# Chunk 0's loop in a hand-written engine order, paired weight conversions and a later output-weight conversion

## The chip, the cores and the metric

The program runs on one core of one Trainium2 chip. The metric is the device time of one execution in microseconds (us). The engines are TensorE (PE in the profile), VectorE (DVE), ScalarE (ACT), GpSimd (POOL) and SyncE (SP), whose queue issues nearly all DMAs.

## The reference, cut to what matters

```python
# 4 x 8 heads, 576 positions, head dim 64; window of 128 keys, linear position bias
scores = where(mask, q @ k.T / 8 + bias, -1e9)
x = softmax(scores) @ v                      # -> 2304 tokens x 512
x = ((x @ w_a) * (x @ w_b)) @ w_out          # float64 weights, 512 x 1536, 512 x 1536, 1536 x 512
logits = x @ w_gate + modality_bias[modality_id]
e = argmax(logits); gate = max softmax prob
out[token] = gate * (relu(x @ w1[e]) @ w2[e])   # 8 experts, 512 x 1024 x 512
```

Products in float32 quality are made of three reduced-precision products (high x high, high x low, low x high), so most operands exist as a high and a low half.

## The kernel before, in words

The 2304 tokens are 18 blocks of 128, grouped into seven **chunks** of 3, 2, 2, 3, 3, 3 and 2 blocks (`CH`, line 43). Attention runs ahead of the product with the gated weights: an **item** is one block of one pair of heads, four pairs to a chunk, so chunk 0 has items 0 to 11 (`n0` is 12), chunk 1 items 12 to 19, and chunk 2 starts with item 20. An item is a score product (`score_mm`), a masked maximum on VectorE (`score_sel`, `score_max`), two exponentials on ScalarE (`score_exp`), the inverse sums on VectorE (`score_inv`), two transposes (`pt_tr`), a copy on ScalarE and two triangular selects on GpSimd (`pt_cp`), the product with the values (`pv_mm`), its scaling out of PSUM (`pv_ev`, tile `u`), and a transpose and copy into the x of the next stage (`pv_tr`, `pv_x`).

The **prologue** (lines 826 to 920) does chunk 0's items in a hand-written order, three items in flight, with the loads and the first weight conversions woven in (`conv_step`).

After it, each chunk runs 12 **steps** j (`NJ`): `mm_ab(c, j, 0)` and `mm_ab(c, j, 1)` are the products with pair j of the weights a and b (12 matmuls each), the result of the first is copied by ScalarE (`asb`), VectorE multiplies it with the second (`gf`), and `mm_out` adds its product with row block j of the output weights to accumulators, one step later. While chunk 0 runs, the weights are made as well. They arrive as float64: per weight, three VectorE operations build the float32 bits (`f64_ops`, lines 452 to 470), ScalarE rounds the high half and VectorE subtracts it for the low half (`f64_split`, line 472). For pair j that is six operations, two casts and two subtractions over 128x512; the output weights need the three operations only, and are written to DRAM for the later chunks (`WoOps`).

What sets the order: chunks 1 to 5 are inside a block in which TensorE, ScalarE and VectorE take the order of the code (`step`, line 1107). Chunk 0's loop (`slot0`, line 1045) is not: there a scheduler with a timeline of its own places instructions, led by priorities (`HP0`, `HPO`) and by `issue_after`. GpSimd and SyncE are always placed by the scheduler, outside the prologue. In `slot0(j)` the output weights of step j + 1 and the pair j + 2 are converted; items go on at eight in twelve steps, and so do the preparations of keys, queries and values of the items ahead (`a_preps`).

## Time and profile before

| | |
|---|---|
| median of 3 runs (lowest, highest) | 841.86 us (840.77, 845.12) |
| profiled execution: its own time, its span | 843.18 us, 840.9 us |
| busy share of the span: PE, DVE, ACT, POOL | 97%, 65%, 55%, 28% |
[...]

The span runs from the first to the last instruction; the rest of the profiled execution's own time lies around it. A busy share is an average over stages with different limits, so the sections below read stretches of the span. A duration in a row includes some 0.1 us in which the next instruction of that engine already runs, so the step from start to start is shorter than the mean of one.

### The profile page before, as it was taken

Reading aid. Unit: us, or ns where it says so; the run is one execution under the profiler, and the core shown is the slowest. Engines: PE = TensorE matmul, PEld = TensorE weight load, DVE = VectorE, ACT = ScalarE, POOL = GpSimd, SP = SyncE. Lnnn points to the kernel's source line nnn. Section 1 sums busy time; section 2 is a strip of 40 time slices with the busy share of each in tenths; the row PEclk is TensorE's granted clock in tenths of the full one; section 3 lists DMA queues with packets and bytes.
Section 4 is the critical chain, followed back from the end, with each engine's and each line's share of the span. In section 5 each row is a group of like instructions: output and inputs, shape, how many; then the busy total and the mean of one; then the engine's idle time right before and its main releaser. Section 6 shows DMA issues by size and latency. Waiting matters only on the chain.

```text
span 840.9 us, 14490 instructions
## 1 busy us (share of the span) xinstructions
PE 813.1 (97%) x4726; PEld 728.0 (87%) x4726; DVE 546.7 (65%) x1619; ACT 461.2 (55%) x1149; POOL 236.1 (28%) x349
## 2 busy tenths in 40 slices
PE   8899999999999999999999999999999999999994
PEld 6788877898898899999999899988988998989893
DVE  7799993677766676767777776468476544447320
ACT  6744453777677766667667643232345443547420
POOL 5422010533344333243333421210133130115001
PEclk9999999999999999999999999999999999999998
DMA  9995443567655675564455544458428564549301
GB/s 252 336 399 193 141 141 113 170 197 230 173 164 152 207 179 154 157 167 136 135 157 152 134 131 119 117 160 272 153 66 305 203 195 136 164 137 295 119 27 40
DMA packets 77348, 144.61 MB, mean 172 GB/s; under 512 B 13839, under 2 KB 40623, under 8 KB 77264
## 3 DMA queue, kind: packets, MB, share of 16 engines
q1 hardware_dynamic: 73712, 133.86, 52.6%
q0 software_dynamic: 3552, 9.73, 3.2%
q8 instruction: 40, 0.66, 0.3%
q14 instruction: 44, 0.36, 0.1%
HBM read 118.16 MB, written 22.12 MB: 167 GB/s over the span
## 4 chain that ended last, share of the span: by engine, by line
PE 65%; DMA 9%; ACT 8%; issue 8%; DVE 5%; POOL 2%; SPq 1%; POOLq 0%; ACTq 0%; DVEq 0%
PE ps_ab L539 26%; PE acc L556 10%; PE ps_h L1291 9%; PE ps_y L1274 8%; PE acc L552 4%; PE ps_o L412 2%; PE ps_s L268 2%; DMA wraw<-in_moe_w_b 2%; ACT u L419 2%; DMA kk<-in_k 1%; ACT p L292 1%; DMA x2d<-x 1%; ACT qq L200 1%; PE ps_p L327 1%; DMA qr<-in_q 1%
## 5 line engine op out<-in xcount | busy, mean ns | idle before, releaser
L539 PE MATMUL ps_ab<-xr,wab 128*128 128x384 f32 (+1 forms) x2016 | 339.2, 318 | 3.3 <-DVE gf L1243 1.6
L539 PEld LDWEIGHTS ps_ab<-xr,wab 128*128 128x128 f32 x2016 | 309.1, 189 | 12.1 <-issue 2.2
L556 PE MATMUL acc<-wo,g 128*128 128x512 f32 x540 | 138.7, 398 | 1.5 <-ACT g L1156 1.5
L556 PEld LDWEIGHTS acc<-wo,g 128*128 128x128 f32 x540 | 96.6, 188 | 20.6 <-ACT g L1156 2.3
L1291 PE MATMUL ps_h<-xT,w1s 128*128 128x384 f32 x576 | 105.7, 340 | 0.0
L1274 PE MATMUL ps_y<-w2s,h 128*128 128x512 f32 x432 | 104.1, 394 | 0.0
L343 POOL TENSOR_SCALAR_AFFINE_SELECT pt<-pc 128x512 fp32r<-128x512 f32 (+1 forms) x72 | 53.8, 747 | 176.0 <-DVE pc L341 109.8
L1291 PEld LDWEIGHTS ps_h<-xT,w1s 128*128 128x128 f32 x576 | 101.1, 190 | 0.9
L1274 PEld LDWEIGHTS ps_y<-w2s,h 128*128 128x128 f32 x432 | 79.7, 188 | 15.8
L292 ACT ACTIVATE p<-p,mx 128x128 f32<-128x128 f32 x144 | 57.0, 398 | 55.1 <-DVE mx L282 55.0
L1144 DVE TENSOR_TENSOR gf<-ps_ab,asb 128x384 f32<-128x384 f32 (+1 forms) x60 | 30.3, 504 | 64.4 <-PE ps_p L327 43.4
L637 DVE CUSTOM_DVE_ANT_0 junk<-x,wgt 128x512 f32<-128x512 f32 x88 | 62.6, 711 | 8.9 <-DMA wgt<-in_wgt 4.2
L423 POOL TENSOR_TENSOR xf<-u 128x128 f32<-128x128 f32 x52 | 25.6, 492 | 128.5 <-ACT u L419 128.5
L310 ACT ACTIVATE p<-p,mx 128x128 f32<-128x128 f32 x104 | 36.5, 397 | 37.2 <-DVE mx L299 37.2
L955 DVE TENSOR_TENSOR w2s<-wr,w2s 128x1024 fp32r<-128x1024 f32 x24 | 29.4, 1225 | 38.4 <-ACT w2s L954 38.1
L1281 POOL DMA_INDIRECT out<-y,idx x18 | 21.2, 1178 | 113.7 <-ACT y L1280 112.2
L419 ACT COPY u<-ps_o 64x384 f32<-64x384 f32 x104 | 49.5, 476 | 3.2 <-PE ps_o L412 2.0
L345 POOL TENSOR_SCALAR_AFFINE_SELECT pt<-pc 128x512 fp32r<-128x512 f32 (+1 forms) x72 | 49.9, 693 | 0.0
L1294 ACT ACTIVATE h<-ps_h 128x384 fp32r<-128x384 f32 x48 | 23.6, 492 | 45.4 <-PE ps_h L1291 43.0
L955 DVE TENSOR_TENSOR w1s<-wr,w1s 128x1024 fp32r<-128x1024 f32 x28 | 34.3, 1224 | 19.0 <-ACT w1s L954 16.3
L1123 ACT COPY asb<-ps_ab 128x384 f32<-128x384 f32 (+1 forms) x60 | 25.9, 431 | 33.9 <-PE ps_ab L539 33.7
L1295 DVE SCALAR_TENSOR_TENSOR h<-ps_h,h 128x384 fp32r<-128x384 f32 x48 | 26.4, 555 | 27.9 <-ACT h L1294 27.9
(224 smaller groups left out, 1231.1 us busy)
## 6 DMA issues: line engine op xcount, KB each, us to landing
wo<-wo_d SPq DMA_DIRECT2D x60, 512.0 KB
wr<-in_moe_w SPq DMA_DIRECT2D x56, 512.0 KB
wgt<-in_wgt SPq DMA_DIRECT2D x32, 256.0 KB
wraw<-in_moe_w_a SPq DMA_DIRECT2D x12, 512.0 KB
wraw<-in_moe_w_b SPq DMA_DIRECT2D x12, 512.0 KB
wor<-in_moe_w_out SPq DMA_DIRECT2D x12, 512.0 KB
wo_d<-wo SPq DMA_DIRECT2D x12, 512.0 KB
kr<-in_k SPq DMA_DIRECT2D x24, 256.0 KB
```

The costliest lines, as they stand in the source:

```text
L292: nc.scalar.activation(out=it.p[:, h, :], in_=it.p[:, h, :], func=AF.Exp, bias=it.mx[:, 2 + h:3 + h], scale=-1.0, accum_out=it.mx[:, 4 + h ...
L310: nc.scalar.activation(out=it.p[:, h, :], in_=it.p[:, h, :], func=AF.Copy, scale=it.mx[:, 6 + h:7 + h])
L343: nc.gpsimd.affine_select(out=it.pt[:, :, 0], in_=pc, pattern=pat + [[-1, P]], base=0, channel_multiplier=1, compare_op=ALU.is_gt, fill=0.0)
L345: mark["pt"] = nc.gpsimd.affine_select(out=it.pt[:, :, 1], in_=pc, pattern=pat + [[1, P]], base=0, channel_multiplier=-1, compare_op=ALU.i ...
L419: nc.scalar.copy(out=u[o:o + 64], in_=ps[o:o + 64, 1 - h:4 - h])
L539: nc.tensor.matmul(ps[:, :n], lhsT=w[:, m, r, kk * P:(kk + 1) * P], rhs=xr[:, s, kk, :n], start=(idx == 0), stop=(idx == len(terms) - 1))
L552: nc.tensor.matmul(acc[c, t], lhsT=g[:, t * P:(t + 1) * P], rhs=w, start=(j == 0), stop=(j == NJ - 1))
L556: nc.tensor.matmul(acc[c, t], lhsT=g[:, r, t * P:(t + 1) * P], rhs=w[:, s, :], start=(j == 0 and idx == 0), stop=(j == NJ - 1 and idx == 2))
L637: nc.vector.tensor_tensor_reduce(out=junk, in0=x2[:, 0:DM], in1=w, scale=1.0, scalar=0.0, op0=ALU.mult, op1=ALU.add, accum_out=lgr[:, e:e ...
L955: nc.vector.tensor_tensor(out=dst[:, 1], in0=srcw, in1=dst[:, 0], op=ALU.subtract)
L1274: nc.tensor.matmul(pss[t], lhsT=h[:, r, f, t * P:(t + 1) * P], rhs=W2[f // 2][:, s_, f % 2, :], start=(f == 0 and i == 0), stop=(f == 7 an ...
L1291: nc.tensor.matmul(ps, lhsT=W1[f // 2][:, r, kk, (f % 2) * P:(f % 2 + 1) * P], rhs=xT[:, s_, kk, :], start=(kk == 0 and i == 0), stop=(kk ...
```

## The change

Chunk 0's loop moves into the hand-ordered block of chunks 1 to 5: `slot0` goes, `step0` takes its place, and the block now opens at chunk 0 (TensorE, VectorE, ScalarE). Both weights of a pair become one tile `f64f` of 128x1024 with one buffer (it shares its place with the later gate weights `wgt`), so that a pair is three conversions, one cast and one subtraction. `step0(j)` converts the output weights of step j - 1 (before: j + 1 in slot j) and loads one step ahead less. The prologue converts pair 0 alone, from its fifth item on (`CVS` 4), and no output weights; pair 1 is converted at the head of step 0. In the prologue both halves of `u` come from ScalarE; before, VectorE made the first. Items and preparations of chunk 0's loop follow a list `goal`, as in the later chunks.

```diff
-    CVS = 1
+    CVS = 4
 def pv_ev(it):
         for h in range(2):
-            if it.a.c == 0 and h == 0:
-                nc.vector.tensor_scalar(out=it.o[:, h], in0=it.po[:, h, 0:D],
-                                        scalar1=it.mx[:, 6 + h:7 + h], scalar2=None, op0=ALU.mult)
-                continue
             nc.scalar.activation(out=it.o[:, h], in_=it.po[:, h, 0:D], func=AF.Copy,
                                  scale=it.mx[:, 6 + h:7 + h])
 def wab_jobs(j):
+        def f():
+            if not st:
+                st.append(m1.tile([P, 2 * KD * P], U32, tag="ff", bufs=1, name="f64f"))
+            return st[0]
+        def hi():
+            wab[j] = wab_p.tile([P, 2, 2, KD * P], F32R, tag=f"wab{j}", name=f"wab{j}")
+            nc.scalar.copy(out=wab[j][:, :, 0], in_=f().bitcast(F32).rearrange("p (m n) -> p m n", m=2))
+        def rest():
+            nc.vector.tensor_tensor(out=wab[j][:, :, 1], in0=f().bitcast(F32).rearrange("p (m n) -> p m n", m=2),
+                                    in1=wab[j][:, :, 0], op=ALU.subtract)
+        return f64_ops(wraw[j].rearrange("p m k f t -> p (m k f) t"), f) + [hi, rest]
...
+    def step0(j, pend, sc, tp):
+        n, last = CH[0] * P, j == NJ - 1
+        new = list(range(cur["s"], goal[j]))
+        its = [live[g] for g in tp]
+        for g in sc:
+            score_inv(live[g])
+        for i in ((1, 2) if j == 0 else (j + 2,)):
+            if i < NJ:
+                job[i] = wab_jobs(i)
+        jo = [f for i in ((j - 1, j) if last else (j - 1,)) if i >= 0 for f in wo_jobs(i)]
+        if j == 0:
+            for f in job.pop(1):
+                f()
+        elif j + 1 in job:
+            job.pop(j + 1)[4]()
+        psa = mm_ab(0, j, 0, None if j else 1)
...
+        nc.scalar.copy(out=asb[:, :n], in_=psa[:, :n])
+        for it in its:
+            xf_new(it.a)
+            pv_mm(it)
+            pv_ev(it)
+        for f in jo:
+            f()
+        js = job.get(j + 2, [])
+        for f in js[:2]:
+            f()
+        psb = mm_ab(0, j, 1)
...
+        nc.vector.tensor_tensor(out=gf[:, :n], in0=psb[:, :n], in1=asb[:, :n], op=ALU.mult)
+        for it in its:
+            pv_tr(it)
+            pv_x(it, 0)
+        for g in sc:
+            pt_tr(live[g])
+        for g in new:
+            c_, hp_, t_ = items[g]
+            live[g] = score_mm(pairs[c_, hp_], t_)
+        for f in js[2:3]:
+            f()
+        for g in sc:
+            pt_cp(live[g])
...
+        for g in new:
+            score_red(live[g])
+            score_exp(live[g])
+        for f in js[3:4]:
+            f()
+        new_preps(goal[j + 2], goal[j])
+        if pend is not None:
+            mm_out(*pend, wo_t[j - 1])
```

Three places of the order. First ScalarE in the prologue, items 3 and 4: `pc` is the transposed weights of an item copied out of PSUM, `p,mx` its exponentials, `u` its scaled product with the values, `xr` the high half of x.

```order
 L333 COPY pc<-ps_p 128x256
 L292 ACTIVATE p,mx<-p,mx 128x128 x2
-L376 ACTIVATE u<-ps_o,mx 128x64
-L392 CAST xr_131<-ps_ot 128x128
-L333 COPY pc<-ps_p 128x256
-L292 ACTIVATE p,mx<-p,mx 128x128 x2
+L372 ACTIVATE u<-ps_o,mx 128x64 x2
+L388 CAST xr_131<-ps_ot 128x128
+L333 COPY pc<-ps_p 128x256
+L292 ACTIVATE p,mx<-p,mx 128x128 x2
```

The order is the same, with two halves of `u` on this engine in the place of one.

Second, VectorE in step 2 of the loop, as it stands now (`f64f` is the pair being converted, `f64o` the output weights, `wor` their raw load, `ps_s` and `p,mx` the new item):

```order
L457 SCALAR_TENSOR_TENSOR f64f<-wraw_209,f64f 128x1024
L276 COPY_PREDICATED ps_s<-upper,ps_s 128x2x128
L282 ISA p,mx<-ps_s,m_base 128x128
L298 TENSOR_SCALAR mx<-mx 128x2
L299 RECIPROCAL mx<-mx 128x2
L483 TENSOR_TENSOR wab_838<-f64f,wab_838 128x2x512
L453 TENSOR_SCALAR f64o<-wor 128x512
L457 SCALAR_TENSOR_TENSOR f64o<-wor,f64o 128x512 x2
L453 TENSOR_SCALAR f64f<-wraw_690 128x1024
L457 SCALAR_TENSOR_TENSOR f64f<-wraw_690,f64f 128x1024
L1056 TENSOR_TENSOR gf<-ps_ab_884,asb 128x384
```

Between the new item's maximum (L282) and the subtraction of the pair (L483) the engine has only the two small operations of the inverse. Before, two pairs were in work at once, and their conversions stood between the parts of an item:

```order
L458 TENSOR_SCALAR f64f<-wraw_716 128x512
L276 COPY_PREDICATED ps_s<-upper,ps_s 128x2x128
L458 TENSOR_SCALAR f64f<-wraw_826 128x512
L462 SCALAR_TENSOR_TENSOR f64f<-wraw_716,f64f 128x512
L282 ISA p,mx<-ps_s,m_base 128x128
L462 SCALAR_TENSOR_TENSOR f64f<-wraw_826,f64f 128x512
L466 SCALAR_TENSOR_TENSOR f64f<-wraw_716,f64f 128x512
L1076 TENSOR_TENSOR gf<-ps_ab_955,asb 128x384
```

Third, ScalarE around steps 0 and 1 as it stands now; `pc` on the second row is item 12, `u` on the fifth too, `qq` the queries of the next pair of heads:

```order
L292 ACTIVATE p,mx<-p,mx 128x128 x2
L333 COPY pc<-ps_p 128x256
L480 CAST wab_720<-f64f 128x2x512
L1044 COPY asb<-ps_ab_649 128x384
L372 ACTIVATE u<-ps_o,mx 128x64 x2
L384 COPY xf_0_728<-ps_o 128x128
L333 COPY pc<-ps_p 128x256
L480 CAST wab_766<-f64f 128x2x512
L242 ACTIVATE qq<-qr_1_695,qscale 64x256 x2
L1044 COPY asb<-ps_ab_779 128x384
```

The cast of a pair (L480), which waits for VectorE's three operations, now stands ahead of `asb` and `u` of the same step.

## Rows read from the trace of the kernel before

**Rows 1.** The page: busy time and share of the span, by engine.
```profile
PE 813.1 (97%) x4726; PEld 728.0 (87%) x4726; DVE 546.7 (65%) x1619; ACT 461.2 (55%) x1149; POOL 236.1 (28%) x349
```

**Rows 2.** Busy time of each engine by stretch, clock, DMA share and GB/s.
```profile
core 0: us, PE busy (x) PEld busy (x) DVE busy (x) ACT busy (x) POOL busy (x), PEclk, DMA share, GB/s
10.00:40.00 30.00, 26.01 (x164) 20.48 (x164) 25.24 (x113) 23.21 (x89) 13.36 (x33) 1.00 1.01 319
...
59.00:142.00 83.00, 83.00 (x406) 66.35 (x405) 72.38 (x167) 37.84 (x103) 10.26 (x13) 1.00 0.49 158
142.00:212.00 70.00, 67.73 (x498) 62.68 (x498) 47.68 (x163) 52.90 (x146) 29.04 (x42) 1.00 0.63 197
```

**Rows 3.** The same view, single stretches around the loop's start.
```profile
40.00:42.00 2.00, 2.00 (x9) 2.00 (x9) 0.57 (x2) 0.47 (x2) 0.00 (x0) 0.50 0.98 384
48.00:50.00 2.00, 0.93 (x5) 0.48 (x4) 2.00 (x4) 2.00 (x8) 0.67 (x2) 1.00 1.02 410
```

**Rows 4.** Timeline of TensorE (start, us, what): chunk 0's first product.
```profile
40.22 3.15 PE L539 MATMUL ps_ab<-xr,wab 128*128 128x384 f32 x9
```

**Rows 5.** The chain that ended last, in order of time (start, us, what).
```profile
55.33 0.11 PE ps_p L327
...
68.83 0.92 PE ps_s L264 x4
...
110.63 0.47 PE ps_s L268 x4
...
118.19 0.84 PE ps_o L366 x8
...
130.10 2.58 PE acc L552 x6
132.67 4.17 PE ps_ab L539 x24
...
141.99 1.44 PE ps_ab L539 x12
```

**Rows 6.** Waits of ScalarE to 142 us: us in total, times, longest.
```profile
ACT u L376 <- DVE u L373: 6.1, 7, 1.3
```

**Rows 7.** Timeline of ScalarE, item 7 of the prologue.
```profile
26.43 0.29 ACT L376 ACTIVATE u<-ps_o,mx 128x64 f32<-128x64 f32 x1
26.62 0.25 ACT L392 CAST xr<-ps_ot 128x128 fp32r<-128x128 f32 x1
27.00 0.37 ACT L333 COPY pc<-ps_p 128x256 f32<-128x256 f32 x1
27.26 0.40 ACT L292 ACTIVATE p<-p,mx 128x128 f32<-128x128 f32 x1
...
28.05 1.13 ACT L473 CAST wab<-f64f 128x512 fp32r<-128x512 f32 x2
30.21 0.32 ACT L376 ACTIVATE u<-ps_o,mx 128x64 f32<-128x64 f32 x1 [1.03 <-DVE u L373]
```

**Rows 8.** Timeline of ScalarE: queries scaled, 64x256 and 64x384.
```profile
23.96 1.26 ACT L242 ACTIVATE kk<-raw,qscale 64x384 f32<-64x384 f32 x2
...
33.03 1.04 ACT L242 ACTIVATE qq<-qr,qscale 64x256 f32<-64x256 f32 x2
```

**Rows 9.** Timeline of GpSimd around the modality constants; then one DMA stretch.
```profile
18.97 0.21 POOL L812 CAST mid<-mid_i 128x18 f32<-128x18 int32 x1
...
21.17 0.40 POOL L343 TENSOR_SCALAR_AFFINE_SELECT pt<-pc 128x256 f32<-128x256 f32 x1
...
16.00:17.00 1.00, 0.56 (x2) 0.37 (x3) 1.00 (x3) 0.97 (x4) 0.00 (x0) 1.00 1.10 18
```

**Rows 10.** Groups of VectorE by form, 59 to 142 us (busy, mean ns).
```profile
L462 DVE SCALAR_TENSOR_TENSOR f64f<-wraw,f64f 128x512 uint32<-128x512 uint32 x17 | 11.3, 687 | 0.0
...
L1076 DVE TENSOR_TENSOR gf<-ps_ab,asb 128x384 f32<-128x384 f32 x11 | 6.0, 550 | 6.6 <-PE ps_ab L539 6.6
...
L276 DVE COPY_PREDICATED ps_s<-upper,ps_s 128x256 f32<-128x256 uint8 x6 | 2.5, 424 | 0.0
...
L282 DVE CUSTOM_DVE_ANT_0 p<-ps_s,m_base 128x128 f32<-128x128 f32 x6 | 1.5, 287 | 0.0
```

**Rows 11.** Timeline of VectorE: two conversions in a row.
```profile
95.89 0.76 DVE L458 TENSOR_SCALAR f64f<-wraw 128x512 uint32<-128x512 uint32 x2
...
97.22 1.29 DVE L462 SCALAR_TENSOR_TENSOR f64f<-wraw,f64f 128x512 uint32<-128x512 uint32 x2
```

**Rows 12.** Groups at 128x1024 in the expert stage, 500 us on, by form.
```profile
L955 DVE TENSOR_TENSOR w1s<-wr,w1s 128x1024 fp32r<-128x1024 f32 x28 | 34.3, 1224 | 19.0 <-ACT w1s L954 16.3 <-issue 2.7
...
L954 ACT CAST w1s<-wr 128x1024 fp32r<-128x1024 f32 x28 | 29.3, 1047 | 17.8 <-DMA wr<-in_moe_w 13.1 <-PE ps_h L1291 4.6
```

More of the change, by code (lines that the diff above doesn't have):

```diff
@@ L394, in pv_x, with xf_new @@
             it.last = nc.vector.tensor_tensor(out=xr[:, 1, a.hp, n], in0=it.px, in1=xr[:, 0, a.hp, n], op=ALU.subtract)
+    def xf_new(a):
+        if a.c > 0 and (a.c, a.hp) not in xf_t:
+            xf_t[a.c, a.hp] = m1.tile([P, MT * P], F32, tag="xf", bufs=KD + 1, name=f"xf{a.c}_{a.hp}")
     def a_pv(it):
         a, t = it.a, it.t
-        if a.c > 0 and (a.c, a.hp) not in xf_t:
-            xf_t[a.c, a.hp] = m1.tile([P, MT * P], F32, tag="xf", bufs=KD + 1, name=f"xf{a.c}_{a.hp}")
+        xf_new(a)
         if a.c in V32:
@@ L450, in attn_moe_moe2, with f64_ops, more @@
     PB = ()
[L452 to L453 removed]
+    def f64_ops(r, f, done=None):
         def one():
[L456 to L458 removed]
+            nc.vector.tensor_scalar(out=f(), in0=r[:, :, 1], scalar1=3, scalar2=0x3FFFFFFF,
                                     op0=ALU.logical_shift_left, op1=ALU.bitwise_and)
[L461 to L474 removed]
+        def more(k, sc, op):
+            nc.vector.scalar_tensor_tensor(out=f(), in0=r[:, :, k], scalar=sc, in1=f(), op0=op, op1=ALU.bitwise_or)
+            if k == 0 and done:
+                done()
+        return [one, lambda: more(1, 0xC0000000, ALU.bitwise_and), lambda: more(0, 29, ALU.logical_shift_right)]
     def wab_load(j):
@@ L843, in attn_moe_moe2 @@
         consts_load()
-        wo_load(0)
         wab_load(1)
         a_loads(n0)
-        wo_load(1)
+        wo_load(0)
         wab_load(2)
         wab_load(3)
-        for j in range(NCV):
-            conv += wab_jobs(j)
-            if j == 0:
-                conv += wo_jobs(0)
+        conv += wab_jobs(0)
         def st(lim, f, g, *x):
@@ L864, in conv_step @@
         def conv_step(g):
-            if g >= CVS and len(conv) > 8:
-                kd = conv[0][0]
-                for _ in range(2 if kd == "s" else 1):
-                    if conv and conv[0][0] == kd:
-                        conv.pop(0)[1]()
+            if g >= CVS and conv:
+                conv.pop(0)()
         ns = n0 + 2
@@ L918, in attn_moe_moe2 @@
         pt_cp(i0)
-        score_inv(i1)
-        score_nrm(i1)
-    for kd_, f in conv:
-        if kd_ == "d" and LA:
-            with tc.issue_after(l1.last.ins):
-                f()
-        else:
-            f()
-    cur = {'s': n0 + 2, 't': n0 + 1, 'o': n0}
-    def upto(w, f, g):
-        while cur[w] < min(g, len(items)):
-            f(cur[w])
-            cur[w] += 1
+    assert not conv
+    cur = {'s': n0 + 2}
     zr = []
@@ L1105, in attn_moe_moe2 @@
     goal += [len(items)] * 2
+    pend = None
+    job = {}
+    def step0(j, pend, sc, tp):
[15 more added lines that the diff above has]
+        for g in sc:
+            score_nrm(live[g])
+        late_rests()
+        asb = m1.tile([P, MT * P], F32, tag="asb", bufs=1, name="asb")
+        nc.scalar.copy(out=asb[:, :n], in_=psa[:, :n])
[9 more added lines that the diff above has]
+        psb = mm_ab(0, j, 1)
+        gf = m1.tile([P, MT * P], F32, tag="g", bufs=2, name="gf")
+        nc.vector.tensor_tensor(out=gf[:, :n], in0=psb[:, :n], in1=asb[:, :n], op=ALU.mult)
[9 more added lines that the diff above has]
+            f()
+        for g in sc:
+            pt_cp(live[g])
+        if last:
+            wo_fetch(0, 1)
+            wo_fetch(1, 1)
+            x_split(1)
+        for g in new:
[6 more added lines that the diff above has]
+            mm_out(*pend, wo_t[j - 1])
+        cur["s"] = goal[j]
+        for g in tp:
+            live.pop(g)
+        return (0, j, gf), new, sc
     def step(c, j, pend, sc, tp):
-        n, k = CH[c] * P, (c - 1) * NJ + j
+        n, k = CH[c] * P, c * NJ + j
         new = list(range(cur["s"], goal[k]))
@@ L1123, in step @@
         nc.scalar.copy(out=asb[:, :n], in_=psa[:, :n])
-        if j == 0 and k:
+        if j == 0 and c > 1:
             evac(c - 1)
```

140 lines of the change are left out of this document (29 added, 111 removed).

## The prediction

> **What bounds the kernel now.** The page comes first: TensorE is busy for 97% of the span [rows 1], but that is an average over stages. The stretches come next [rows 2]. From 59 to 142 us, in chunk 0's loop, TensorE works all 83.0 us and VectorE 72.4 of them; nothing there is gained by taking work off VectorE, and something is lost only where TensorE has to wait for it. From 10 to 40 us, the prologue, no engine is full (TensorE 26.0, VectorE 25.2, ScalarE 23.2 of 30, the clock full): there a chain of waits between engines sets the pace. So the change is costed at two places, the prologue up to T0, the start of the loop's first product (40.22 [rows 4]), and the loop up to chunk 1's first product (141.99, last row of [rows 5]): 101.8 us.
>
> What TensorE must do in the loop, from the durations in the chain [rows 5]: a step has 24 products for a pair (4.17) and the accumulation (2.58), 6.75 in all, by 12 steps 81.0. Eight items' products with the values, .84 and a transpose of .11 each, give 7.6; the score products (seven of .92, two of .47) 7.4; ten pairs of transposes of weights at .22 2.2. Together 98.2. At the head the granted clock is .50 [rows 3], and nine products take 3.15 [rows 4] where half of that would do: 1.6 more, 99.8. The kernel before thus loses only 2.0 us of the loop to waits, of which 1.1 lie between 48 and 50, where TensorE is busy .93 of 2.00 [rows 3].
>
> **Prologue, -4.0 us.** The first half of `u` moves from VectorE to ScalarE. ScalarE waited 6.1 us in seven waits for that half [rows 6]; one of them is the 1.03 us ahead of 30.21 [rows 7], behind conversions of weights. The waits go; the added half costs a step of .19 (26.43 to 26.62 [rows 7]), 2.3 for twelve items. VectorE loses twelve halves and the conversions of the output weights, and so is late nowhere. The next late engine is GpSimd: it stands at a constant until 18.97 and makes item 4's selects at 21.17 [rows 9], and in 16 to 17 us the DMA engines are full at only 18 GB/s [rows 9], which I read as that constant's small packets. I take it to land by some 17.9 (an estimate: a microsecond after that row), as the loads ahead of it are no shorter; 2.2 us on, the distance in before, selects of item 4 are at 20.2, 1.0 earlier.
>
> From there to T0 before takes 40.22 - 21.17 = 19.05 us for the last items. After it, ScalarE is the longest: per item a copy .26, exponentials .79, two halves of `u` .38, x .25 (starts and ends in [rows 7]), 1.68, by seven items 11.8; keys 1.26 and queries 1.04 [rows 8], one cast of a whole pair 1.05 [rows 12]: 15.1. With half a microsecond of waits at each end, my choice between none and before's longest of 1.3 [rows 6], 16.1. T0 comes at 20.2 + 16.1 = 36.3, so -3.9 to -4.0. The bounds: only the constant's -1.0 if the waits change their releaser alone; and -5.4 if ScalarE too is off the path, since TensorE's own work (.92 + .22 + .95 = 2.09 an item [rows 5]) is 14.6 for seven items.
>
> **Loop, +3.6 us.** The merged operations first. Two conversions of 128x512 in a row take 1.29 [rows 11], one operation on 128x1024 takes 1.22 [rows 12]: .07 is saved for each of four operations per pair, nearly nothing. It is the order that matters. VectorE's round in a step, by start-to-start times: `gf` .47 and the third conversion 1.14; select and maximum of the new item up to ScalarE's start .65; ScalarE's exponentials .79; the cast, behind them, 1.10; only then the subtraction 1.14; the output weights .33 + .60 + .60; two conversions of the next pair .65 + 1.14. That is 8.6 us with a new item (seven steps of ten) and 7.2 without, 8.2 in the mean; TensorE's 98.2 over 12 steps are 8.2 too. Neither engine has room for the other's delay. (`gf` .55, select .42 and maximum .29 as in [rows 10], less the tenth that overlaps; 1.14 and 1.05 from [rows 12], the first conversion .76 for two [rows 11].) Before, two pairs were in work and conversions filled the time of the exponentials.
>
> I walked the first steps through the new orders. Step 0: pair 1 is now converted and cast inside the step, ahead of item 12's `u` on ScalarE; TensorE finishes its products and the score of item 13 at T0 + 4.0, the copy of item 12's weights is at 5.8 and GpSimd's selects (.41 apiece) end at 6.4 and 7.2, so TensorE stands about 2.2. `u` of item 12 is behind pair 1's cast (VectorE's three operations 6.5 to 8.8, cast to 9.9): the pair's high half is there at 9.9, the low at 11.0, .7 more. Step 1: item 13's `u` stands behind pair 2's cast and the queries (1.04), 1.3. In steps 2 and 3 the accumulation waits for the output weights, which are now converted in the step before use, .65 and .6; a last .3 in step 9. That is 5.6 to 5.7 against 2.0: +3.6 as the walk rounds. After step 1 the lag of VectorE is taken up by TensorE's own, so later steps cost little. The bounds: +1.6, if only step 0's 2.2 and .7 and half of step 1's stand; +6.8, if VectorE's round is .3 longer than reckoned over ten steps, as it is when its operations keep their lone length (.687 [rows 10]) and do not overlap.
>
> **Costed at nothing.** SP issues one output-weight load fewer ahead and the pair loads as before; the DMA share is .49 in the loop [rows 2], and pairs 6 and 7, now behind four other loads, are needed some 40 us later. If that cover went, a pair of float64 weights would stop a step. One pair of heads' preparations (keys, queries, values: 2.4 us on ScalarE, 2.4 on VectorE) moves to chunk 1, where ScalarE works 52.9 and VectorE 47.7 of 70 us [rows 2]: 0, with 2.4 as the end if it lands on that chunk's chain. The gate weights in one tile keep their loads and order: 0.
>
> **Sum.** The profiled execution takes 843.18 us, 840.9 of it span, 1.3 above the median of 841.86. -4.0 + 3.6 = -0.4: 842.8 on its own time, 841.5 on the median. My own range for this case is 839 to 844.
>
> **Rivals.**
>
> *VectorE's round bounds the loop (slower).* It decides as soon as the round is longer than 8.2 us in the mean, because there is no stock of converted weights left at T0: one pair in the place of one and a half, and no output weights. For it: 8.6 in a step with an item. Against: 7.2 in the others. Priced at the upper end, loop +6.8; and if pair 1's conversion at the head finds its operands no earlier than TensorE wants them, half of the prologue's gain goes: -2.0. Together +4.8, 846.7. Chance .24.
>
> *The prologue gives all and the loop little back (faster).* ScalarE off the path, -5.4, and +1.6: 838.1; should TensorE also enter the loop at full clock, 1.6 less, 836.4. For it: ScalarE was busy only 23.2 of 30 us [rows 2]. Against: it now has 1.68 an item and the cast, keys and queries besides. Chance .22.
>
> *A second stretch at half clock.* Where TensorE stood before T0, nine products took 3.15 [rows 4] at clock .50 [rows 3]. If step 0's stops of 2.2 and .7 do it again, some 1.1 is lost once more: 842.6. [...] Against, by rows: between 48 and 50 TensorE was busy less than half, and the granted clock stayed at 1.00 [rows 3]. Chance .07.
>
> *The change does not do what it says in the prologue.* The waits for `u` only become waits for GpSimd's selects: -1.0 and +3.6, 844.5. For it: GpSimd is at most one item ahead. Chance .06.
>
> *Merged operations shorten VectorE's round.* If an operation on 128x1024 followed the next without the gap that a pair shows, the two halves at .687 [rows 10] against 1.224 [rows 12] save .15, not .07, four times a pair: .3 to .4 us a step, and the stops of steps 2, 3 and 9 (1.6) vanish: 839.9. [...] Chance .04.
>
> **How the numbers follow.** Forecast .37, the rivals .24, .22, .07, .06 and .04. A measurement of this kernel can tell about 0.5%, 4.2 us, from no change: 837.7 and 846.1 are the bounds. Faster takes nine tenths of the second rival's .22, since its own values lie between 836.4 and 838.1 and an extra gain is as likely as a missing one: .20. Slower takes most of the first rival (.20) and .02 of each of the fourth's and the forecast's tails: .23. The rest is .57. The range must hold 836.4 and 846.7 and some of what lies beyond: 835.5 to 848.0, where the upper end is the fourth rival's prologue (-1.0) with the loop's worst (+6.8): 847.7. The likeliest case's own range stays 839 to 844.
>
> **What will show it.** Right: T0 at 36 to 37; no wait of ScalarE for `u`; in step 0 a wait of TensorE of about 2 us for GpSimd's selects; VectorE waiting for ScalarE's cast before each subtraction, which it did not before; accumulations waiting for output weights in steps 2 and 3; chunk 1's first product at 141 to 142. Wrong: T0 at 39 or later (prologue), or TensorE waiting for VectorE's low halves in the steps beyond 3 (the first rival), or no stops in step 0 (the second), or clock .50 after 50 us (the third). Chunk 1 longer than 70 us for the same work would mean that the moved preparations cost something.

## The result and the profile after

The changed kernel takes 852.41 us (median of 4 runs, 850.87 to 854.96) against 841.61 in the same runs: ratio 1.0123, interval 1.0085 to 1.0161. It is slower; 841.5 was forecast, with 848.0 as the upper end. The profiled execution of the changed kernel took 850.87 us with a span of 848.9, that of before 843.18 with 840.9, so the traces hold 8.0 us of the 10.8 between the medians; the rest is the spread between executions of one kernel.

The windows of the changed kernel, by stage, answer to [rows 2, 3] (the same columns):

```profile
20.00:30.00 10.00, 8.32 (x49) 7.47 (x49) 5.49 (x20) 6.81 (x25) 4.33 (x9) 0.83 1.05 387
30.00:40.00 10.00, 9.28 (x66) 8.08 (x66) 6.09 (x30) 8.90 (x41) 4.32 (x12) 1.00 0.97 347
40.00:50.00 10.00, 6.79 (x32) 6.16 (x31) 7.02 (x16) 3.25 (x10) 2.85 (x4) 0.83 1.03 412
...
38.64:149.77 111.13, 102.23 (x490) 80.93 (x489) 91.39 (x168) 41.45 (x114) 16.99 (x22) 0.98 0.50 175
149.77:848.90 699.13, 675.73 (x4046) 619.78 (x4044) 429.99 (x1257) 390.64 (x929) 199.65 (x267) 0.99 0.53 162
```

The same stages in the kernel before:

```profile
40.22:141.43 101.21, 100.14 (x490) 80.79 (x489) 88.10 (x213) 45.39 (x130) 15.61 (x22) 0.99 0.59 203
141.43:840.90 699.47, 678.52 (x4046) 621.16 (x4044) 425.94 (x1249) 387.37 (x919) 200.38 (x267) 0.99 0.54 161
```

The end of the loop is chunk 1's first product, read from TensorE's timeline in both kernels. Before, that is 141.43:

```profile
141.43 2.00 PE L539 MATMUL ps_ab<-xr,wab 128*128 128x256 f32 x12
```

The 141.99 of [rows 5], which the prediction took, is where the chain's row begins, cut off by the accumulation ahead of it; the same product starts .56 us before.

The loop starts 1.6 us earlier (38.64 against 40.22 [rows 4]) and is 9.9 longer (111.13 against 101.21); chunk 1's first product comes at 149.77 in place of 141.43, 8.3 later. Of the 9.9 us, 7.8 are idle time of TensorE (111.13 - 102.23 = 8.9 against 101.21 - 100.14 = 1.07) and 2.1 are more busy time. The clock explains little of these 2.1: each loop holds one stretch at half clock, 3.4 us now and 3.0 before.

What follows takes the same time in sum (699.1 and 699.5), but not stage by stage. Chunk 1, before and after:

```profile
141.43:212.04 70.61, 68.34 (x501) 63.01 (x499) 47.72 (x163) 53.23 (x147) 29.08 (x42) 1.00 0.62 196
149.77:223.54 73.77, 69.98 (x500) 63.47 (x499) 51.48 (x171) 57.36 (x157) 29.76 (x42) 1.00 0.64 200
```

It is 3.2 us longer now; chunks 3, 4 and 5, each from its first product to the next one's, are .7, .8 and .6 shorter and the rest 1.4, which hides it.

TensorE's timeline (start, us, what, and the idle time ahead with its releaser) shows where:

```profile
18.60 0.38 PE L327 MATMUL ps_p<-ident,p 128*128 128x128 f32 x2
21.68 1.88 PE L366 MATMUL ps_o<-raw,pt 128*128 128x64 f32 x8 [2.70 <-POOL pt L343]
23.35 0.42 PE L379 MATMUL ps_ot<-ident,u 128*128 128x128 f32 x1
23.57 1.91 PE L264 MATMUL ps_s<-kk 128*128 128x256 f32 x4
...
38.64 1.81 PE L534 MATMUL ps_ab<-xr,wab 128*128 128x384 f32 x9
...
44.47 0.43 PE L366 MATMUL ps_o<-vv,pt 128*128 128x64 f32 x2 [2.30 <-POOL pt L343]
45.81 1.37 PE L366 MATMUL ps_o<-vv,pt 128*128 128x64 f32 x6 [0.91 <-POOL pt L345]
46.94 3.49 PE L534 MATMUL ps_ab<-xr,wab 128*128 128x384 f32 x12
...
50.51 2.34 PE L534 MATMUL ps_ab<-xr,wab 128*128 128x384 f32 x12
...
128.55 2.84 PE L547 MATMUL acc<-f64o,gf 128*128 128x512 f32 x6 [2.03 <-DVE f64o L457]
```

Item 4's product with the values waits 2.70 us for GpSimd, and the score product behind it takes 1.91 where the later ones take 1.03. In the loop step 0 waits 2.30 and .91 for item 12's selects, and twelve products take 3.49 where the next take 2.34. From some 22 to 25.5 us and from 46 to 49.5 us the granted clock is at .50 (two of these microseconds):

```profile
23.00:24.00 1.00, 1.00 (x6) 0.91 (x6) 0.00 (x0) 0.59 (x4) 0.25 (x1) 0.50 1.14 348
...
47.00:48.00 1.00, 1.00 (x4) 1.00 (x4) 0.06 (x1) 1.00 (x2) 0.00 (x0) 0.50 1.03 410
```

So the half-clock stretch that stood at the loop's head [rows 3] is gone from there (nine products take 1.81 us, 3.15 before), but there are two others now, each behind a stop of TensorE. The waits of the loop, TensorE's and then VectorE's (what waited for what: us, times, longest):

```profile
PE acc L547 <- DVE f64o L457: 5.3, 6, 2.0
PE ps_o L366 <- POOL pt L343: 2.3, 1, 2.3
PE ps_o L366 <- POOL pt L345: 0.9, 1, 0.9
...
DVE wab L483 <- ACT wab L480: 9.0, 11, 1.1
DVE mx L298 <- ACT p L292: 5.6, 8, 0.7
```

Before, VectorE waited .2 us for ScalarE's casts in the whole loop. Now it idles 14.6 us for casts and exponentials, and TensorE waits six times for output weights, 5.3 us in all. One round of VectorE, with a new item, from product to product of `gf`:

```profile
68.02 0.55 DVE L1056 TENSOR_TENSOR gf<-ps_ab,asb 128x384 f32<-128x384 f32 x1
68.49 1.21 DVE L457 SCALAR_TENSOR_TENSOR f64f<-wraw,f64f 128x1024 uint32<-128x1024 uint32 x1
69.62 0.42 DVE L276 COPY_PREDICATED ps_s<-upper,ps_s 128x256 f32<-128x256 uint8 x1
...
71.32 0.17 DVE L298 TENSOR_SCALAR mx<-mx 128x2 f32<-128x2 f32 x1 [0.73 <-ACT p L292]
...
72.26 1.23 DVE L483 TENSOR_TENSOR wab<-f64f,wab 128x1024 fp32r<-128x1024 f32 x1 [0.57 <-ACT wab L480]
73.40 0.42 DVE L453 TENSOR_SCALAR f64o<-wor 128x512 uint32<-128x512 uint32 x1
73.86 1.42 DVE L457 SCALAR_TENSOR_TENSOR f64o<-wor,f64o 128x512 uint32<-128x512 uint32 x2
75.19 0.69 DVE L453 TENSOR_SCALAR f64f<-wraw 128x1024 uint32<-128x1024 uint32 x1
75.91 1.31 DVE L457 SCALAR_TENSOR_TENSOR f64f<-wraw,f64f 128x1024 uint32<-128x1024 uint32 x1
77.14 0.55 DVE L1056 TENSOR_TENSOR gf<-ps_ab,asb 128x384 f32<-128x384 f32 x1
```

Every gap in the round is a wait for ScalarE, and the round repeats: `gf` starts 9.32 us apart in steps with an item (68.02 from 58.70, 94.06 to 103.38, 103.38 to 112.70; the round shown takes 9.12) and 7.59 without. TensorE needs 8.2 in the mean.

### The profile page after: what moved, and what is told of

Read it like the earlier page. It is cut to its first block, busy times and chain, and to the rows that moved or that the text cites. A ratio compares the mean times of both kernels' runs of the same rounds, so it can differ in the third digit from the quotient of the medians.

```text
span 848.9 us, 14452 instructions
## 1 busy us (share of the span) xinstructions
PE 811.3 (96%) x4726; PEld 727.7 (86%) x4726; DVE 547.6 (65%) x1559; ACT 460.3 (54%) x1149; POOL 236.5 (28%) x349
## 4 chain that ended last, share of the span: by engine, by line
PE 52%; DVE 14%; ACT 12%; issue 12%; DMA 5%; POOL 3%; SPq 0%; POOLq 0%; ACTq 0%; DVEq 0%
PE ps_ab L534 20%; PE acc L551 10%; PE ps_y L1250 8%; PE ps_h L1267 7%; ACT p L292 2%; PE ps_o L411 2%; PE ps_s L268 2%; DVE f64f L457 2%; DVE f64o L457 2%; ACT u L418 1%; ACT wab L480 1%; ACT qq L200 1%; PE ps_p L327 1%; DVE pc L341 1%; DVE f64f L453 1%
## 5 line engine op out<-in xcount | busy, mean ns | idle before, releaser
L551 PE MATMUL acc<-wo,g 128*128 128x512 f32 x540 | 136.0, 393 | 1.6 <-ACT g L1135 1.6
L422 POOL TENSOR_TENSOR xf<-u 128x128 f32<-128x128 f32 x52 | 25.5, 491 | 109.6 <-ACT u L418 109.5
```

The costliest lines, as they stand in the source:

```text
L551: nc.tensor.matmul(acc[c, t], lhsT=g[:, r, t * P:(t + 1) * P], rhs=w[:, s, :], start=(j == 0 and idx == 0), stop=(j == NJ - 1 and idx == 2))
```

## The experiments

Theory: VectorE's round in series with ScalarE bounds the loop, and the prologue's gain is lost at GpSimd's constants. T0 is the loop's first product, T1 chunk 1's first product, both from the profiled execution (us), and the loop is T1 - T0. The ratio is against runs of before on the same chip. The medians come from several chips, on which the kernel before took 841.6 to 843.2, so differences of 1 or 2 us between them are read from the ratios and their intervals. The profiled execution was the longest of its kernel's in e3, e7 and e14 and the shortest in the changed kernel and e13.

| kernel | T0 | T1 | loop | median us | ratio (interval) |
|---|---|---|---|---|---|
| before | 40.22 | 141.43 | 101.2 | 841.6 | 1 |
| changed | 38.64 | 149.77 | 111.1 | 852.4 | 1.0123 (1.0085 to 1.0161) |
| e1 output weights first | 38.67 | 143.97 | 105.3 | 846.9 | 1.0052 (1.0035 to 1.0068) |
| e2 constants late | 35.19 | 149.20 | 114.0 | 852.6 | 1.0116 (1.0093 to 1.0139) |
| e3 u split again | 40.84 | 152.41 | 111.6 | 855.3 | 1.0150 (1.0127 to 1.0172) |
| e4 before, u on ScalarE | 38.29 | 139.66 | 101.4 | 841.1 | 0.9979 (0.9962 to 0.9996) |
| e5 e1 + step 0's products | 39.04 | 144.11 | 105.1 | 845.7 | 1.0029 (1.0015 to 1.0044) |
| e6 e5 + constants late | 35.17 | 143.59 | 108.4 | 845.8 | 1.0034 (1.0019 to 1.0050) |
| e7 interleaved | 39.40 | 151.06 | 111.7 | 853.2 | 1.0111 (1.0087 to 1.0135) |
| e8 unmerged | 38.57 | 152.74 | 114.2 | 854.6 | 1.0142 (1.0120 to 1.0165) |
| e9 e6 + pair 1 in the prologue | 39.71 | 143.78 | 104.1 | 845.3 | 1.0029 (1.0011 to 1.0048) |
| e10 e6 + a buffer | 35.20 | 138.61 | 103.4 | 840.7 | 0.9976 (0.9957 to 0.9995) |
| e11 e9 and e10 | 38.83 | 142.10 | 103.3 | 844.7 | 1.0019 (0.9995 to 1.0043) |
| e12 e4 + constants late | 38.87 | 139.78 | 100.9 | 842.2 | 0.9986 (0.9962 to 1.0009) |
| e13 e10 + pair 1 in the gaps | 35.55 | 136.00 | 100.5 | 836.1 | 0.9933 (0.9907 to 0.9960) |
| e14 changed, step 0 alone | 39.45 | 148.77 | 109.3 | 850.5 | 1.0097 (1.0071 to 1.0123) |

**e1: output weights at the head of VectorE's step.**

```diff
+        for f in jo:
+            f()
         for g in sc:
             score_inv(live[g])
...
             pv_ev(it)
-        for f in jo:
-            f()
```

> The changed kernel with one edit: in each step of chunk 0's loop the three output-weight conversions stand at the head of VectorE's step, ahead of the inverse sums and of the pair's subtraction, instead of behind them. Theory 1 (VectorE's round of 9.3 us in a step with an item, 7.6 without, sets the loop, because VectorE idles 14.6 us behind ScalarE's exponentials and cast): the 1.9 us of conversions fill that idle time of 0.6 + 0.7 or 1.1 us a step, the round falls to some 8.0 and 6.5, under TensorE's 8.2; TensorE's 5.3 us of waits for output weights fall under 1; chunk 1's first product comes 4 to 5 us earlier (145 to 146), the time is 4 to 5 us below the changed kernel's 852.4. Rival (the round is set by operations in a row that depend on each other, or by TensorE's stops of step 0, and the waits only move to the low halves of the pairs): less than 1.5 us, and TensorE waits for wab instead.

As theory 1 has it: 5.5 us less, T1 at 143.97. TensorE no longer waits for output weights, VectorE's wait for casts falls from 9.0 to 1.1 and for exponentials from 5.6 to 1.2, and the same step's round is 7.67 (68.10 to 75.77) in place of 9.12. Half of the loss is the order of three operations. TensorE's stops of step 0 (2.30 and .91) are as they were, and a wait for `u` at 74 us grows from .26 to 1.73. What takes the waits' place on VectorE:

```profile
DVE f64o L453 <- PE acc L547: 4.0, 4, 1.1
...
DVE f64o L453 <- DMA wo_f<-f64o: 2.3, 1, 2.3
```

**e2: constants three items later** (`CJ = 3` becomes 6).

> The changed kernel with GpSimd's routing constants three items later in the prologue (behind item 6's selects instead of item 3's). Theory 2 (the prologue gains only 1.6 us because GpSimd stands until 17.7 us for the constants' load, TensorE has no work for 2.7 us and then runs 4 us at clock 0.50, which costs 2 more): no stop of TensorE over 1 us between 19 and 22, clock 1.00 from 20 to 30, the loop's first product 3 to 4.5 us earlier than 38.6, the time 3 to 4.5 us below the changed kernel. Rival (the constants' 2.3 us of GpSimd work itself, or ScalarE, sets the prologue): first product at 37.5 or later, time within 1.5 us of the changed kernel's.

Half right. T0 is 3.45 us earlier, with no such stop and a clock of 1.00 from 20 to 30. But T1 moves by .6 and the time not at all: the earlier start is lost again in the loop, in a wait of 2.61 for output weights with the clock at .91 in the mean from 60 to 80 and 4.54 us for the accumulation behind it (2.74 for the next).

**e3 and e4: u on VectorE again; u on ScalarE in the kernel before.**

```diff
         for h in range(2):
+            if it.a.c == 0 and h == 0:
+                nc.vector.tensor_scalar(out=it.o[:, h], in0=it.po[:, h, 0:D],
+                                        scalar1=it.mx[:, 6 + h:7 + h], scalar2=None, op0=ALU.mult)
+                continue
             nc.scalar.activation(out=it.o[:, h], in_=it.po[:, h, 0:D], func=AF.Copy,
```

(e4 takes the same four lines out of the kernel before.)

> The changed kernel with the first half of u in the prologue back on VectorE. Theory 2: the shift of u to ScalarE is what brings items 0 to 3 forward by 2 us, and the stop behind the constants eats it; undone, T0 is at 39 to 40.5, with no half-clock stretch at 22 to 26, and the time within 2 us of the changed kernel. Rival (the shift is worth its whole 1.6 us or more at the end): T0 over 40.5 and the time 1.6 to 4 us above the changed kernel.

> The kernel before with one edit: both halves of u come from ScalarE in the prologue. Theory 2: the waits of ScalarE for u (6.1 us) go, but items 0 to 3 then meet the constants' load as in the changed kernel; T0 at 38.5 to 40 and a time 0 to 2 us below the kernel before. Rival (the shift is worth what was forecast): T0 at 36 to 37 and 3 to 4 us below; other rival (worth nothing): T0 at 40 or later.

Undoing it puts T0 at 40.84 and the median 2.8 us up (the rival of e3, though the intervals of the two ratios overlap; the stop at the constants is still there, 1.67 and .92, with a clock of .83 in the mean from 20 to 30). Doing it alone gains 1.4 us with T0 at 38.29 (theory 2's time in e4, with T0 a little ahead of its 38.5). The shift of `u` is worth some 2 us at T0 in either kernel, not the 4 forecast for the prologue.

**e5 and e6: step 0's products reordered; the constants late as well.**

```diff
+        psb = mm_ab(0, j, 1) if j == 0 else None
         for it in its:
             xf_new(it.a)
...
-        psb = mm_ab(0, j, 1)
+        psb = psb if j == 0 else mm_ab(0, j, 1)
```

> The kernel of the first experiment (output weights at the head of VectorE's step) with one more edit: in step 0 TensorE takes the second half of pair 0's products (12, 2.33 us) ahead of item 12's product with the values, so that it has work while the weights of item 12 are copied and selected. Theory 3 (what is left of the loss, 4.4 us above the kernel before, is step 0: 3.2 us of waits for GpSimd's selects and half-clock products behind them, because the exponentials of item 13 and the copy of item 12 stand one behind the other): waits of step 0 under 1 us, no half clock from 46 to 50, chunk 1's first product 3 to 4.5 us earlier than 143.97, the time 843 to 844. Rival (VectorE's round takes it back: pair 1 is converted in step 0 only from 43.5 us on, so TensorE waits for pair 1 in step 1 instead): under 1.5 us earlier, with a wait of TensorE for wab or an idle time before step 1.

> The kernel of the run before this one and the constants three items later, as in the second experiment. Theory 3: in the second experiment the loop's first product came 3.45 us earlier and all of it was given back, since VectorE's round was the bound and the loop's stops set off half-clock stretches; with both out of the way, the 3 us should now reach the end: 840 to 841. Rival (the loop is bound from its start by the loads of float64 weights, which come at the same times whatever T0 is): no change beyond 1 us against the run before, and waits of VectorE for raw weights or for DMA.

Both times the rival came. In e5 the 2.30 us for the first select become .22 (the .91 for the second stays), and 2.07 us of waiting for `u`, behind pair 1's cast, stand a little later. In e6 T0 is 3.9 us earlier than in e5 and T1 only .5: VectorE stands at a conversion of output weights for a DMA. Its timeline, and SP's queue:

```profile
62.55 0.43 DVE L453 TENSOR_SCALAR f64o<-wor 128x512 uint32<-128x512 uint32 x1 [5.75 <-DMA wo_f<-f64o]
```

```profile
49.31 0.33 SPq L466 DMA_DIRECT2D wraw<-in_moe_w_b  x1
50.63 0.33 SPq L466 DMA_DIRECT2D wraw<-in_moe_w_a  x1
51.87 0.33 SPq L466 DMA_DIRECT2D wraw<-in_moe_w_b  x1
53.21 0.38 SPq L178 DMA_DIRECT2D vv<-in_v  x1
54.49 0.33 SPq L507 DMA_DIRECT2D wo_f<-f64o  x1
```

The output weights of the step before were converted by 51.2; their store is issued at 54.49, behind the last loads of pairs, which SP lets go one in 1.2 to 1.4 us while the DMA engines are full (share 1.03 at 402 GB/s from 50 to 60 us). VectorE goes on at 62.55, once the store has landed: its buffer is the one that the next conversion wants (e10 tests that).

**e7: conversions interleaved; e8: conversions of a pair halved again.**

```diff
-        for f in jo:
-            f()
         js = job.get(j + 2, [])
-        for f in js[:2]:
-            f()
+        for k in range(max(len(jo), 2)):
+            for f in jo[k:k + 1] + js[k:min(k + 1, 2)]:
+                f()
```

```diff
-            nc.vector.scalar_tensor_tensor(out=f(), in0=r[:, :, k], scalar=sc, in1=f(), op0=op, op1=ALU.bitwise_or)
+            for s in hv:
+                nc.vector.scalar_tensor_tensor(out=f()[:, s], in0=r[:, s, k], scalar=sc, in1=f()[:, s], op0=op, op1=ALU.bitwise_or)
```

(`hv` are the two halves; the first conversion likewise.)

> The changed kernel with one edit: the output-weight conversions and the first two conversions of the next pair alternate on VectorE, so that hardly any of these five operations reads what the one just before it wrote. Theory 4 (a VectorE operation that reads the result of the one before it starts only after that one has ended, .13 us later than an independent one, and this is why the round is 9.3 instead of the 8.6 reckoned): some .35 us less in the round of each step, 3 to 4 us less over ten steps, the time 848 to 850. Rival (the round's excess comes from GpSimd's selects or from waits for semaphores): within 1 us of the changed kernel's 852.4, the five operations taking as long as before (3.9 us from the first's start to the end of the last).

> The changed kernel with one edit: each conversion of a pair is two operations of 128x512 again, one for each weight, next to each other; cast and subtraction stay whole. It takes back the merging alone. Theory 4: the two halves do not depend on each other, so they cost what the row of two in a row showed (1.29 against 1.22), and GpSimd's selects are held up half as long (.86 in place of 1.39): step 0's wait for the selects .5 us shorter, the round within .1, the time within 2 us of the changed kernel. Rival (the fixed cost of an operation counts in full): .15 for each of three operations a step, 4 to 5 us slower than the changed kernel.

In e7 the mechanism is there and the time is not. The five operations, in e7:

```profile
73.30 0.42 DVE L453 TENSOR_SCALAR f64o<-wor 128x512 uint32<-128x512 uint32 x1
73.63 0.69 DVE L453 TENSOR_SCALAR f64f<-wraw 128x1024 uint32<-128x1024 uint32 x1
74.23 0.69 DVE L457 SCALAR_TENSOR_TENSOR f64o<-wor,f64o 128x512 uint32<-128x512 uint32 x1
74.84 1.22 DVE L457 SCALAR_TENSOR_TENSOR f64f<-wraw,f64f 128x1024 uint32<-128x1024 uint32 x1
75.97 0.69 DVE L457 SCALAR_TENSOR_TENSOR f64o<-wor,f64o 128x512 uint32<-128x512 uint32 x1
76.57 0.55 DVE L1055 TENSOR_TENSOR gf<-ps_ab,asb 128x384 f32<-128x384 f32 x1
```

In these rows an independent operation starts .08 to .09 before the end of the one ahead (73.30 + .42 = 73.72, next at 73.63); one that reads the result of the one ahead starts .03 to .04 after it (73.40 + .42 = 73.82, next at 73.86 in the round shown above). The five take 3.27 us to `gf`, against 3.74 there, and `gf` comes 8.66 apart in steps with an item. Of the .47, three dependent places make .37 or so; the rest is the last conversion, which took 1.31 there beside one of GpSimd's selects and 1.22 here. So e7's rival is right as well in part: in the steps of 9.32 two conversions beside the selects are .30 longer:

```profile
100.82 0.75 POOL L343 TENSOR_SCALAR_AFFINE_SELECT pt<-pc 128x256 f32<-128x256 f32 x1 [7.76 <-ACT pc L333]
101.53 0.85 POOL L345 TENSOR_SCALAR_AFFINE_SELECT pt<-pc 128x256 f32<-128x256 f32 x1
```

```profile
101.22 0.89 DVE L453 TENSOR_SCALAR f64f<-wraw 128x1024 uint32<-128x1024 uint32 x1
102.15 1.31 DVE L457 SCALAR_TENSOR_TENSOR f64f<-wraw,f64f 128x1024 uint32<-128x1024 uint32 x1
```

(These are the changed kernel's; in its steps without an item the two take .69 and 1.22.) But in e7 the last conversion of the output weights ends behind the pair's, TensorE still waits 4.9 us for them, and one such wait (2.06) is followed by an accumulation of 4.54 us (2.74 or 2.84 in the steps before; the clock is .92 in the mean from 120 to 142). That the round alone decides falls here: what TensorE waits for is the output weights, and those came later. In e8 a round is 9.53 in place of 9.32, .07 for each of three operations as [rows 11, 12] say; the median is 2.2 us above the changed kernel's, by the ratios (1.0142 and 1.0123) 1.6, about theory 4's 2 and under half of its rival's 4 to 5 (the rival's .15 an operation is 2 x .687 [rows 10] - 1.224 [rows 12]). Step 0's wait for the selects falls from 3.2 to 2.0 us, as GpSimd's four operations from 40 to 50 us take 1.75 in place of 2.85 (the changed kernel's selects .89 and 1.39 of it), but 1.43 of waiting for `u` come behind it.

**e9, e10, e11: pair 1 in the prologue; a buffer more; both.**

```diff
-    CVS = 4
+    CVS = 1
...
-        conv += wab_jobs(0)
+        conv += wab_jobs(0) + wab_jobs(1)
...
```

(Step 0 then leaves out its conversion of pair 1.)

```diff
-                wo_t[j] = m1.tile([P, DM], U32, tag="wo", bufs=WOB, name="f64o")
+                wo_t[j] = m1.tile([P, DM], U32, name="f64o", **(dict(tag="fo", bufs=1) if j % 2 else dict(tag="wo", bufs=WOB)))
```

> The last combination (output weights first, second half of pair 0 ahead in step 0, constants late) with pair 1 converted in the prologue, as in the kernel before, instead of at the head of step 0. Theory 5 (the 5 us between the combination and what its earlier start promises are two stops: u of item 12 behind pair 1's cast, 2.07 us with 1.3 us of half clock behind it, and VectorE's 5.8 us behind the store of output weights): the first goes, step 0 has no stop over 1 us and no half clock at 46 to 50; the first product of the loop comes up to 1 us later (one more cast of 1.05 on ScalarE); the wait for the store stays or grows, and so does TensorE's wait for output weights in step 2; time 843 to 846. Rival (VectorE has no room in the prologue, so T0 moves by 3 us or more): 846 or over.

> The last combination (without pair 1 in the prologue) with one more buffer: the converted output weights alternate between the shared buffers and one of their own. Theory 5: VectorE's 5.8 us wait at 62 us is for the buffer of the output weights before, whose store to DRAM stands in SP's queue behind nine loads of pairs; with a buffer of its own the wait goes, TensorE's 2.95 us wait in step 2 and the half clock behind it too; chunk 1's first product 3 to 4.5 us earlier than 143.6, the time 841 to 843. Rival (what VectorE really waits for is a raw load, or the loads of pairs set the pace to 62 us anyhow): within 1 us of 845.8, with the wait under another name.

> Both edits of the two runs before this one. Theory 5: both stops gone, chunk 0's loop at 100 to 102 us from a first product at 35 to 36.5, chunk 1's first product at 136 to 138, the time 836 to 839, under the kernel before. Rival (loads bound the first steps: 24 loads of 512 KB at 400 GB/s end at 62 us whatever the engines do): a stop of TensorE for wab before 62 us, and 841 or over.

e10 is theory 5: the DMA wait is gone, T1 5.0 us earlier, the time 5.1 lower and .24% under the kernel before. In e9 the stop for `u` falls to .61, but T0 is 4.5 later than in e6, as its rival has it (the time, 845.3, is in theory 5's range): from 20 to 30 us VectorE works 9.59 of 10, so it has little room for pair 1's four operations ahead of the items' own work. That is not shown alone, since `CVS` moves the conversions from the fifth item to the second as well; from 10 to 20 us VectorE works 6.89 there and 7.50 in e6. Nor does e9 go back to the kernel before, as its text says: there pair 1 is converted behind T0, from 44.03 on. In e11 the buffer takes away a wait of 2.0 for the store that e9 still has, and T1 comes 1.7 earlier than in e9; the late T0 stays, and theory 5's 836 to 839 is missed.

**e12: the constants late in e4** (`CJ = 6`).

> The kernel before with both halves of u from ScalarE in the prologue and the constants three items later; its loop stays with the scheduler. Theory 2 (the prologue's 4 us are real once nothing stands at the constants): first product of the loop at 35.5 to 37 and the time 838 to 840, 3 to 4 us below the kernel before. Rival (the half-clock stretch and the loads give it back): 841 or over.

The rival's time, 842.2, but not for its reason: T0 is at 38.87, later than e4's 38.29, so there was no earlier start for a half-clock stretch to give back. With twelve conversions of 128x512 in its prologue (e2 has three of 128x1024) the constants are not what holds it. So the 35.2 of e2 seems to need both: conversions merged and put off, and nothing standing at the constants.

**e13 and e14: pair 1 in VectorE's gaps.** VectorE idles about a microsecond before each of the last halves of x (1.05, .91 and 1.04 in the changed kernel); pair 1's conversions go there, the copy of item 12 ahead of item 13's exponentials, and item 12's inverse ahead of item 13's maximum.

```diff
         pv_x(live[n0 - 3], 1)
+        j1[0]()
...
         pv_x(l1, 0)
+        j1[1]()
         pv_x(l1, 1)
...
         pt_tr(i0)
-        score_exp(i1)
         pt_cp(i0)
+        score_exp(i1)
+        j1[2]()
```

(The cast and subtraction of pair 1 follow `asb` in step 0. e13 is e10 with this; e14 is the changed kernel with this and e5's edit.)

> The best combination so far (output weights first, second half of pair 0 ahead in step 0, constants late, one more buffer: 840.7) with step 0 mended in another way: pair 1's three conversions stand in the gaps that VectorE has between the last halves of x at the end of the prologue, the copy of item 12's weights ahead of item 13's exponentials, asb ahead of pair 1's cast. Theory 6 (what is left of step 0's loss is that pair 1 is converted only from 43.5 us on, and so u of item 12 and pair 1's products late): T0 stays at 35 to 35.5, step 0's stops fall from 3.2 us to under 1, no half clock after them, chunk 1's first product at 135 to 136.5, the time 837 to 838.5. Rival (DMA sets the first steps: the 24 loads of pairs end at some 60 us): the stops reappear as waits for wab or a raw load before 62 us, and the time stays within 1 us of 840.7.

> The changed kernel with the step-0 edits alone (pair 1's conversions in the gaps at the prologue's end, copy of item 12 ahead of item 13's exponentials, second half of pair 0 ahead of the product with the values); output weights, constants and buffers as changed. Theory 6: the chain of VectorE's rounds starts some 3 us earlier and the half clock of step 0 goes, so 3 to 4 us of the changed kernel's 10.8 us loss are step 0's: 848 to 849.5, with the waits for output weights (5.3 us) as they were. Rival (the rounds behind it decide alone): within 1.5 us of 852.4.

e13 takes 836.1 us, .67% under the kernel before and clear of its spread. Its loop and TensorE's waits in it:

```profile
35.55:136.00 100.45, 98.37 (x490) 79.63 (x489) 90.42 (x170) 42.66 (x114) 15.31 (x22) 1.00 0.61 210
```

```profile
PE ps_o L379 <- ACT u L372: 2.0, 2, 1.4
```

98.37 us of products at full clock (98.2 were reckoned) and 2.0 of waits: nothing is left in this loop but the two waits for `u`. The granted clock is 1.00 over the loop and from 600 to 640 us; the traced execution of before has half clock at 40 us and again from 616.6 to 620.0 (.50 in each full microsecond there), and the latter lies outside what the edit touches, so a part of the .67% may not be the edit's. e14 gains 1.9 by the medians, between theory 6 (3 to 4) and its rival (under 1.5), and 1.0 at T1; the intervals of its ratio and the changed kernel's overlap. Step 0's waits for the selects and the half clock there are gone (two waits for `u`, .61 and 1.36, remain), but the next output weights then wait 1.66 for the store, and TensorE 2.69 for them at 65.67, with an accumulation of 4.38 behind it (2.74 for the next; the clock is .91 in the mean from 60 to 80).

## Why the prediction was wrong, step by step

**What bounds the kernel**: right. TensorE's 98.2 us for the loop is what e13 shows.

**Prologue, -4.0**: measured -1.6 (38.64 - 40.22). The constant landed at 17.72 (17.9 reckoned) and item 4's selects started at 20.24 (20.2). What failed is "after it, ScalarE is the longest ... with half a microsecond of waits at each end". Items 0 to 3 came 2 us earlier, so everything met at the constant: ScalarE stood 3.30 us behind item 4's selects, TensorE 2.70, and TensorE then lost up to 1.7 us at half clock (.83 over the 10 us from 20 on). And the select itself took 1.39 in place of .41, beside a VectorE conversion. e2 shows the step without the constant: 35.19, 5.0 under before; e4 shows that `u` alone is worth 1.9 (1.4 in e12). In the sum I priced the constant's delay and not what its stop does to TensorE's clock, though the rival of a second half-clock stretch stood in the text for step 0.

**Step 0**: 2.2 reckoned, 2.30 and .91 measured. The half clock behind it, rival at .07, came too: twelve products 1.15 longer. Not each stop has it behind it: the 2.03 us ahead of 128.55 are followed by 2.84, at a granted clock of 1.00.

**VectorE's round**: reckoned 8.6 and 7.2, measured 9.32 and 7.59. This is the step that failed, and with it the sentence that rests on it, "later steps cost little". The terms came from rows in which the scheduler had put operations of different pairs next to each other; in the new order nearly every operation reads the one ahead, and each such place costs .12 to .13. From start to start the three output-weight operations took 1.79 (1.53 reckoned) and the first conversion of a pair .72 (.65): .33 in every round. In steps with an item GpSimd's selects ran beside the conversions of the next pair, which then took .93 and 1.23 in place of .72 and 1.14: .30 more. Neither was in the sum. That the merging saves .07 an operation was right (e8).

**"Later steps cost little"**: wrong, and by the forecast's own condition. The first rival was to decide once the round is over 8.2 in the mean; (7 x 9.3 + 3 x 7.6) / 10 = 8.8. TensorE's six waits for output weights are 5.3 us where the forecast had 1.6 in steps 2, 3 and 9. What those waits hang on is where the output weights stand in the round and not its length alone: with them at its head they are gone (e1, 5.5 us), with the round at 8.66 and the weights no earlier they are not (e7). What came was that first rival. It was priced at +4.8, with a round longer by .3 and not by .7, and with half of the prologue's gain left (2.0; it was 1.6). Its premise on the stock at T0 was read wrongly: before, one pair was ready there too, since pair 1's conversion begins at 44.03; what it had more was the output weights of two steps.

**Costed at nothing**: the preparations moved to chunk 1 cost something there, by the sign that the prediction gave (chunk 1 longer than 70 us): 73.8 against 70.6, with ScalarE 4.1 and VectorE 3.8 us busier. The end that it named, 2.4, came and more (3.2); in e1 to e14 chunk 1 takes 72.8 to 73.8 with the new loop and 70.2 with the old (e4, e12). The total does not show it because chunks 3 to 5 are 2.1 shorter in sum, for a reason that no run here tests, and because before has 3.4 us of half clock from 616.6 on that the changed kernel lacks. The gate weights show no cost. SP's queue, wrong where VectorE is faster: in e1, e6 and e14, among others, the store of the output weights lands late and is waited for (2.3, 5.8, 1.7 us); in the changed kernel there is no such wait.

So the change puts -1.6 and +9.9 where -4.0 and +3.6 were forecast. The prologue's idea is sound and pays 4.7 us at T0 once the constants are moved and pair 1 stays out of its way (e13); the loop's idea does no worse than the scheduler's order (100.5 us against 101.2, of which some 1.5 were lost to half clock) once VectorE has work to do while ScalarE makes exponentials and casts, and once pair 1 is ready at T0; chunk 1 then takes back 2.2 (72.8 against 70.6).

## What to carry to other kernels

When an order that a scheduler interleaved is written by hand, walk one round of each engine with dependent steps and with what runs beside them on the other engines, not with durations from interleaved rows; compare the mean round with the bound's, and see where in the round stands what the bound engine wants next; a round in series over two engines must have independent work placed in each wait. An engine that runs ahead because a wait was removed meets the next fixed event (here a landing constant, then a store behind a queue of loads): move those with it, or the gain stops there. A stop of the bound engine can be worth more than its length: behind step 0's 2.30 and .91 us the granted clock was .50, and twelve products took 3.49 us in place of 2.34.

## What the runs showed of the hardware

- On VectorE, in e7's rows and in the changed kernel's round, an operation that reads what the one ahead wrote starts .03 to .04 us after its end, an independent one .08 to .09 before it; five operations took 3.27 interleaved and 3.74 in order, of which .09 is a select beside the last.
- GpSimd's select on 128x256 takes .41 us alone (37.42 in the changed kernel), and up to 1.39 beside a VectorE conversion of 128x1024 in the changed kernel:

```profile
44.37 1.39 POOL L345 TENSOR_SCALAR_AFFINE_SELECT pt<-pc 128x256 f32<-128x256 f32 x1
```

```profile
44.19 2.65 DVE L457 SCALAR_TENSOR_TENSOR f64f<-wraw,f64f 128x1024 uint32<-128x1024 uint32 x2
```

  The select ends at 45.76, .26 after the first of the two conversions has ended (44.19 + 1.31). Beside one conversion of 128x512 it took .86 in the kernel before (49.69), and up to 1.65 beside several in a row (71.36). So in these rows the select is .98 us longer beside a merged operation and .45 beside a half (1.39 - .41 against .86 - .41). VectorE's operation is longer too: .89 for .69 in the rows of e7's section.
- The same stop is followed by half clock in one run and not in the next: 2.03 us ahead of the same accumulation, then 2.84 us for it in the changed kernel (clock 1.00) and 4.54 in e2 (.93 in the mean from 120 to 145 us).
